# First FFN1 blocks of pair 1 ahead of w1's second half, one transfer for the last weight rows, and LayerNorm of pairs 6 and 7 in the second stage

## The chip, the cores and the metric

The kernel runs on one core of one Trainium2 chip. The metric is device time in microseconds (us) of one execution; the runs of a kernel are given by their median. A profile is one execution recorded by the hardware profiler: its span is the time from the first to the last instruction.

## The reference

Two blocks share one LayerNorm of `A_x` (1 x 2048 x 448, bfloat16) and are added to it; `B_x` is not used.

```python
x  = A_x
xn = layernorm(x)                                   # over 448, eps 1e-5
return x + A(xn, wqkv, w_phi, wo) + B(xn, w1, w2)

# A: linear attention, 16 heads of 28, softmax feature maps
q, k, v = split(xn @ wqkv)
pq, pk  = q @ w_phi, k @ w_phi                      # per head
phi_q   = concat(softmax(pq), softmax(-pq))
phi_k   = concat(softmax(pk), softmax(-pk))
kv, z   = sum_s phi_k v, sum_s phi_k
o       = (phi_q kv) / (phi_q z + 1e-6)
A       = o @ wo
# B: feed-forward, 448 -> 1792 -> 448
B       = silu(xn @ w1) @ w2
```

## The kernel before

The 2048 tokens are cut into 8 **pairs** of 256 tokens. Tokens 2i and 2i+1 of a pair lie in the two tiles t = 0 and 1, on the same partition. Every matmul over the 448 columns contracts seven blocks of 64 rows, and each runs on one half of TensorE's rows: tile 0 on partitions 0 to 63, tile 1 on partitions 64 to 127, both halves at once (`mm_448`, L497). So each weight must be present in both halves. A load (`load_main`, L566) brings rows 0 to 383 as three slots of 128 partitions. `swap` (L575) then copies each half's 64 partitions to the other half, slots 3 to 5, on ScalarE (ACT) or VectorE (DVE). The last 64 rows, 384 to 447, the **tail**, go to slot 6 of both halves by two transfers of 64 rows (`load_tail`, L569).

The work has three stages, which TensorE runs through as one stream:

1. LayerNorm of all pairs (`ln_pair`, L672: bn_stats L621, aggregate L629, ve L635, rstd on POOL L637, normalisation xn L650, then a transpose, for pairs 0 to 3 on TensorE with an eviction by DVE at L668, for pairs 4 to 7 by DMA, L561); the FFN1 blocks of the first pairs (`ffn1_chunk`, L692; 14 blocks of 128 of the 1792 columns, each unit followed by a silu on ACT); and `fold` (L727), which multiplies w_phi into the q and k weights.
2. `k_macro` (L791) for each pair: k matmul, exponentials on ACT, v matmul, v copy (L800), sums Sk and reciprocals Rk on DVE, product phik on POOL (L808); `q_group` (L829), which takes four pairs at a time; and the accumulation of kv (L812). The second group of pairs, 4 to 7, is first read by `q_group` at the fifth pair. At the end, DVE forms KVZ (L854, L855, L862), with a mask of heads.
3. The rest of FFN1, attention output, FFN2 and wo, pair by pair, then the output.

In stage one the first two pairs go as follows. FFN1 blocks 0 to 7 are done for pair 0 alone, since w1 arrives in pieces: w1_0 (columns 0 to 255), w1_0b (256 to 511), w1_1 (512 to 1023), w1_2a (1024 to 1407), w1_2b (1408 to 1791), with tails w1_0t (0 to 511, on ACT's queue) and w1_1t (512 to 1791, on SP's queue behind w1_1). Blocks 8 to 13 are done for pairs 0 and 1 together, and after them blocks 0 to 7 of pair 1. On SP's queue follow x2, x3, w_phi, transposed loads of the q and k weights (wT), x4, x6 and wv.

The order of the instructions on each engine is not written out by hand. A **planner** (`_Prog.schedule`, L218) lists operations with an estimated duration, takes the earliest that can start, and among those within 60 ns the one with the lower priority number and then the earlier place in the program. Loads without a predecessor get a due time from a model of the queues: the end of their bytes at 310 (190 for half transfers) bytes per ns, plus 1700 ns. The resulting order is fixed; on the chip each engine runs its list in order and waits on semaphores. `odeps` are extra order constraints between operations of one engine. Filler matmuls on a tile of zeros (`warm`, L548) have the lowest priority and go where the planner sees nothing else for TensorE.

Of the kernel before, what the change touches and what calls it, by code (L numbers as in the profile page):

```python
# [144 lines left out]
class _Prog:  # L145
# [72 lines left out]
    def schedule(self):  # L218
# [28 lines left out]
        plan = {}  # L247
# [6 lines left out]
        while loads["sp"] or loads["act"]:  # L254
            live = [e for e in ("sp", "act") if loads[e] and loads[e][0][2] <= now]
            nxt = [loads[e][0][2] for e in ("sp", "act") if loads[e] and loads[e][0][2] > now]
            if not live:
                now = min(nxt)
                continue
            cap = [190.0 if ops[loads[e][0][0]].half or ops[loads[e][0][0]].name == "wT_dt" else 310.0 for e in live]  # L260
            rates = [min(c, 310.0 * c / sum(cap)) for c in cap]
            step = min(min(loads[e][0][1] / r for e, r in zip(live, rates)), min(nxt) - now if nxt else 1e18)
            now += step
            if now > 2350.0 and not stalled:
                stalled = True
                now += 900.0
            for e, r in zip(live, rates):
                q = loads[e][0]
                q[1] -= step * r
                if q[1] <= 1.0:  # L270
                    plan[q[0]] = now + 1700.0
                    loads[e].pop(0)

        ndeps = [len(o.deps) + len(o.odeps) for o in ops]
# [90 lines left out]
def bass_parallel_sum__linear_kernel_hedgehog__dense_activation_silu__prompt_kernel(  # L365
# [20 lines left out]
    with es:  # L386
# [141 lines left out]
                                                           base=DH - 1, channel_multiplier=-1),  # L528
             reads=[mtmp[:]], writes=[maskh[:]], name="mask2")
        P.cur_prio = 2  # L530
        for r in range(2):
            P.op("dve", 150, lambda e, r=r: e.tensor_copy(mask2[64 * r:64 * r + 56, :], maskh[0:56, 0:2]),  # L532
                 reads=[maskh[0:56, 0:2]], writes=[mask2[64 * r:64 * r + 56, :]], name="mask3")
        for r in range(2):
            kvz_ones = KVZ[64 * r:64 * r + 56].rearrange("p s g h c -> p (s g) h c")[:, :, :, DH + 1]
            m2 = mask2[64 * r:64 * r + 56]
            P.op("dve", 150, lambda e, k=kvz_ones, m2=m2: e.tensor_copy(k, m2[:, None, :].broadcast_to([56, 8, 2])),  # L537
                 reads=[m2], writes=[kvz_ones], name="kvz1")
        wpad = W_sb[:, :, 0:QW].rearrange("p k (j f) -> p k j f", f=64)[:, :, :, 56:64]
        P.op("pool", d_pool(KB * 64), lambda e: e.memset(wpad, 0.0), writes=[wpad], name="wpad")  # L540

# [3 lines left out]
        zz = sb("zz", [128, 512], BF16)  # L545
        for c0, c1 in ((0, 32), (32, 512)):
            P.op("dve", 450 + (c1 - c0) * 0.3, lambda e, c0=c0, c1=c1: e.memset(zz[:, c0:c1], 0.0), writes=[zz[:, c0:c1]], name="zz")
        for n, rows, cols, dur in ((12, 128, 512, 430.0), (0, 128, 512, 215.0), (14, 128, 256, 109.0)):  # L548
            for i in range(n):
                mm(banks[5][0:rows, 0:cols], zz[:, 0:rows], zz[:, 0:cols], True, True, "warm")  # L550
                P.ops[-1].dur = dur
        P.cur_prio = 0

        def load(dst, src, nbytes, name, eng="sp", keys_r=(), half=False):
            return P.dma(lambda e: e.dma_start(out=dst, in_=src), nbytes, writes=[dst], name=name, eng=eng, keys_r=keys_r, half=half, dur=580.0)
# [10 lines left out]
        def load_main(dst, src, c0, c1, d0, name):  # L566
            load(dst[:, 0:3, d0:d0 + c1 - c0], src[0:384, c0:c1].rearrange("(k p) f -> p k f", p=128), 384 * (c1 - c0) * 2, name)

        def load_tail(dst, src, c0, c1, d0, name, eng="sp"):  # L569
            for h in range(2):  # L570
                o = load(dst[64 * h:64 * h + 64, d0:d0 + c1 - c0], src[384:448, c0:c1], 64 * (c1 - c0) * 2, name, eng, half=True)
                if eng == "act":
                    o.odeps.add(table_op.id)

        def swap(dst, c0, c1, engs):  # L575
            for h in range(2):
                d, q = dst[64 * h:64 * h + 64, 3:6, c0:c1], dst[64 - 64 * h:128 - 64 * h, 0:3, c0:c1]
                if engs[h] == "act":
                    act(d, q, ACTF.Identity, "swap")
                else:  # L580
                    P.op("dve", d_dve(3 * (c1 - c0), 2), lambda e, d=d, q=q: e.tensor_copy(d, q), reads=[q], writes=[d], name="swap")
# [4 lines left out]
        load_x(1, 2)  # L586
        load_main(w1_sb, B_w1, 256, 512, 256, "w1_0b")
        load_main(w1_sb, B_w1, 512, 1024, 512, "w1_1")
        load_tail(w1_sb[:, 6], B_w1, 512, FF, 512, "w1_1t")
        load_main(w1_sb, B_w1, 1024, 1408, 1024, "w1_2a")  # L590
        load_main(w1_sb, B_w1, 1408, FF, 1408, "w1_2b")
        load_x(2, 3)
        load_x(3, 4)
# [51 lines left out]
        def ln_norm(p, t):  # L645
            sl = p % NXN
            dst = xn_sb[:, sl, :].rearrange("p (k t c) -> p k t c", k=KB, t=2)[:, :, t % 2, :]
            for xs, xn in slots(x_sb[:, t, :], dst, t % 2):
                pool = p >= 4 and t % 2
                o = P.op("pool" if pool else "dve", 150 + _cols(xs) * 1.6 if pool else 120 + _cols(xs) * 0.6, lambda e, xn=xn, xs=xs: e.tensor_scalar(  # L650
                    xn, xs, mv[:, t, 0:1], rstd[:, t:t + 1], ALU.subtract, ALU.mult),
                    reads=[xs, mv[:, t, 0:1], rstd[:, t:t + 1]], writes=[xn], name="xn")
                if t < 2:
                    first_xn.append(o)
                    if not pool and t == 0:
                        o.odeps.add(first_ve[1])
# [15 lines left out]
        def ln_pair(p):  # L672
            t0, t1 = 2 * p, 2 * p + 1
            ln_stats(t0)
            if p == 0:
                ln_rstd(t0, t1)
                ln_stats(t1)
                ln_rstd(t1, t1 + 1)
            else:
                ln_stats(t1)  # L680
                ln_rstd(t0, t1 + 1)
            ln_norm(p, t0)
            ln_norm(p, t1)
            ln_tr(p, 6)
# [80 lines left out]
        swap(w1_sb, 768, 1024, ("act", "dve"))  # L765
        ffn1_chunk(0, 1, 4, 8)
        last_mm[-1].odeps |= {q.id for q in second_tr}
        n0 = len(P.ops)
        swap(w1_sb, 1024, 1408, ("act", "dve"))
        second_ev[0].odeps.add(P.ops[-1].id)  # L770
        n0 = len(P.ops)
        swap(w1_sb, 1408, FF, ("act", "dve"))
        P.ops[-1].odeps |= {q.id for q in second_ev}
        ffn1_chunk(0, 2, 8, FT)
        ln_pair(2)
        ffn1_chunk(1, 1, 0, 8)
        ln_pair(3)
        fold()
        ffn1_chunk(2, 1, 0, 8)
        ln_pair(4)  # L780
        ffn1_chunk(2, 2, 8, FT)
        ffn1_chunk(3, 1, 0, 8)
        ln_pair(5)
        ln_pair(6)
        ln_pair(7)

        def k_unit(p, j, b0, name):
            mm_448([banks[b0 + t][:, 0:D] for t in range(2)], lambda h, k: xnT[:, k, p, :],
                   lambda h, k: W_sb[:, k, KO + (j - 1) * D:KO + j * D], True, True, name + "_mm", okeys_w=("late",) if p == NPAIR - 1 and j == 2 else ())

        def k_macro(p):  # L791
            sl = p % NEK
            k_unit(p, 1, 0, "pk")
            kb = psum[:, 0:1024].rearrange("p (t c) -> p t c", t=2)[:, :, 0:D]
            for s in range(2):
                exp_act(Ek[:, sl, :, s, :], kb, 1.0 if s == 0 else -1.0, "exp_k")
            k_unit(p, 2, 2, "v")
            vb = psum[:, 1024:2048].rearrange("p (t c) -> p t c", t=2)[:, :, 0:D].rearrange("p t (h d) -> p t h d", h=H)
            dstv = vaug[:, sl, :, :, 0:DH]
            P.op("dve", d_dve(896), lambda e: e.tensor_copy(dstv, vb), reads=[vb], writes=[dstv], name="v_ev")  # L800
            for ts in ((0, 2),) if p < NPAIR - 1 else ((0, 1), (1, 2)):
                n = ts[1] - ts[0]
                E3 = Ek[:, sl, ts[0]:ts[1], :, :].rearrange("p t s (h f) -> p (t s h) f", f=DH)
                S3, R3 = Sk[:, sl, 32 * ts[0]:32 * ts[1]], Rk[:, sl, 32 * ts[0]:32 * ts[1]]
                P.op("dve", d_dve(896 * n), lambda e, S3=S3, E3=E3: e.tensor_reduce(S3, E3, AXL.X, ALU.add),  # L805
                     reads=[E3], writes=[S3], name="Sk")
                P.op("dve", d_rec(32 * n), lambda e, S3=S3, R3=R3: e.reciprocal(R3, S3), reads=[S3], writes=[R3], name="Rk")  # L807
                P.op("pool", d_pool(896 * n, 1.77), lambda e, E3=E3, R3=R3, n=n: e.tensor_tensor(  # L808
                    E3, E3, R3[:, :, None].broadcast_to([128, 32 * n, DH]), ALU.mult),
                    reads=[E3, R3], writes=[E3], name="phik")  # L810
# [27 lines left out]
                 writes=[vaug[:, sl, :, :, DH]], name="vaug1")  # L838
        for p in range(NPAIR):
            k_macro(p)  # L840
            if 1 <= p <= 5:
                P.keyw["early"] = exps[-1].id
                late_loads(p - 1)
            q_group(p // 4, p % 4)
            if p in (2, 4, 6):
                k_acc(p - 2, p)
# [275 lines left out]
```

## Time and profile before

| | |
|---|---|
| median of 3 runs | 158.16 us (157.37 to 158.72) |
| profiled execution, its own time | 157.24 us |
| its span | 155.5 us |
| TensorE busy | 150.7 us (97%) |
| VectorE busy | 102.6 us (66%) |
| ScalarE busy | 74.2 us (48%) |
| POOL busy | 63.7 us (41%) |
| granted TensorE clock | 1.00 |
| DMA | 12.11 MB, mean 78 GB/s over the span |

"L490" in the profile is the body of `mm_many`, from which nearly all matmuls are issued; "L483" is `mm`, which issues the fillers and the last FFN2 matmuls; "L508" the transposes on TensorE; "L515" every ACT operation; "L581" the swaps on DVE; "L555" every plain load. A busy TensorE is not one at its peak. Idle time of an engine costs only where another engine waits for it.

### The profile page before, as it was taken

The page shows a single profiled execution, that of the slowest core. Times are in us where ns is not written, and L with a number is a line of the kernel's source. Part 1 is how long each engine was busy: PE and PEld are TensorE (multiplying, and loading weights), DVE is VectorE, ACT ScalarE, POOL GpSimd, SP SyncE. Part 2 cuts the span into 40 slices and gives each one's busy share as a digit, 9 for nine tenths or more (in the row PEclk, how much of TensorE's full clock was granted, in tenths as well). Part 3 has the DMA queues.
Part 4 walks back from the last instruction along what each step waited for, and adds up shares of the span by engine and source line. Part 5 has one row for each costly group of instructions (what it writes and reads, how often), then busy time and mean ns, then how long its engine had stood idle before and what let it go on. Part 6 is the DMA issues. An engine that isn't in the chain of part 4 may idle for free.

```text
span 155.5 us, 6049 instructions
## 1 busy us (share of the span) xinstructions
PE 150.7 (97%) x2751; PEld 98.3 (63%) x2751; DVE 102.6 (66%) x198; ACT 74.2 (48%) x82; POOL 63.7 (41%) x73
## 2 busy tenths in 40 slices
PE   6889999999999999999999999999999999999994
PEld 2378899795444546446878898655555555556553
DVE  5897977995978875889098769667985930022042
ACT  3778757878789688785955566800000000000000
POOL 5320306379388775479601453366146060000000
PEclk9999999999999999999999999999999999999999
DMA  5999678303724223300000083300840143041011
GB/s 152 268 277 115 110 180 249 62 17 69 99 53 139 49 93 95 93 0 6 4 4 4 0 63 63 59 4 0 124 118 4 28 115 98 0 118 63 0 59 59
DMA packets 23353, 12.11 MB, mean 78 GB/s; under 512 B 16160, under 2 KB 23200, under 8 KB 23328
## 3 DMA queue, kind: packets, MB, share of 16 engines
q1 hardware_dynamic: 23168, 11.60, 34.9%
q8 instruction: 21, 0.34, 0.9%
q10 hardware_dynamic: 160, 0.13, 0.3%
q14 instruction: 4, 0.03, 0.1%
HBM read 6.22 MB, written 1.84 MB: 52 GB/s over the span
## 4 chain that ended last, share of the span: by engine, by line
PE 89%; DVE 7%; POOL 2%; issue 1%; POOLq 0%
PE psum L490 84%; PE psum L483 4%; PE psum L508 1%; DVE st L621 1%; POOL rstd L637 1%; DVE KVZ L862 1%; DVE kvs L854 1%; DVE kvs L855 1%; DVE mask L532 1%; DVE xn_sb L650 1%; DVE mv L629 0%; DVE xnT L668 0%; DVE ve L635 0%; DVE KVZ L537 0%; POOL ident L519 0%
## 5 line engine op out<-in xcount | busy, mean ns | idle before, releaser
L490 PE MATMUL psum<-xnT,w_sb 64*128 64x256 bf16 (+1 forms) x1008 | 45.6, 246 | 0.5 <-DVE xn_sb L650 0.5
L490 PEld LDWEIGHTS psum<-xnT,w_sb 64*128 64x128 bf16 x1008 | 39.2, 94 | 5.0 <-ACT w_sb L515 0.6
L515 ACT ACTIVATE ar<-psum 128x896 bf16<-128x896 f32 (+2 forms) x38 | 32.0, 880 | 10.9 <-PE psum L490 10.8
L916 POOL TENSOR_TENSOR scr<-scr 128x384 bf16<-128x384 f32 (+3 forms) x32 | 20.1, 660 | 31.8 <-DVE scr L911 26.0
L808 POOL TENSOR_TENSOR ar<-ar,Rk 128x1792 bf16<-128x1792 bf16 (+1 forms) x9 | 25.8, 2877 | 10.1 <-DVE Rk L807 9.1
L960 DVE TENSOR_TENSOR out_sb<-psum,x_sb 128x448 bf16<-128x448 f32 (+2 forms) x17 | 9.5, 593 | 23.6 <-PE psum L490 20.5
L490 PE MATMUL psum<-ar,xnT 64*128 64x448 bf16 x224 | 22.7, 349 | 0.0
L490 PE MATMUL psum<-w_sb,hT_lo 64*128 64x448 bf16 x224 | 22.3, 349 | 0.0
L515 ACT ACTIVATE eq<-psum 128x1024 bf16<-128x1024 f32 x16 | 15.5, 1025 | 6.1 <-PE psum L490 6.0
L805 DVE TENSOR_REDUCE Sk<-ar 128x64 f32<-128x1792 bf16 (+1 forms) x9 | 16.2, 1804 | 2.5 <-ACT ar L515 2.5
L490 PEld LDWEIGHTS psum<-ar,xnT 64*128 64x128 bf16 x224 | 10.7, 94 | 10.4 <-DVE ar L800 0.4
L911 DVE TENSOR_TENSOR scr<-psum,Gq 128x896 f32<-128x896 f32 x16 | 16.9, 1087 | 0.4
L515 ACT ACTIVATE hT_lo<-psum 128x1024 bf16<-128x1024 f32 x14 | 14.3, 1022 | 5.9 <-PE psum L490 5.9
L490 PE MATMUL psum<-w_sb,ar 64*128 64x448 bf16 x168 | 16.6, 349 | 0.0
L490 PEld LDWEIGHTS psum<-w_sb,hT_lo 64*128 64x128 bf16 x224 | 10.5, 94 | 9.4
L637 POOL TENSOR_TENSOR rstd<-ve,neghalf 128x2 f32<-128x2 f32 (+1 forms) x9 | 6.2, 690 | 21.3 <-DVE ve L635 18.9
L490 PE MATMUL psum<-xnT,ar 64*128 64x512 bf16 x112 | 13.4, 376 | 0.0
L490 PEld LDWEIGHTS psum<-w_sb,ar 64*128 64x128 bf16 x168 | 8.4, 94 | 7.4
L490 PE MATMUL psum<-wo_sb,scr 64*128 64x448 bf16 (+2 forms) x119 | 11.9, 338 | 0.0
L800 DVE CAST ar<-psum 128x896 bf16<-128x896 f32 x8 | 8.6, 1069 | 4.0 <-PE psum L490 4.0
L621 DVE BATCH_NORM_STATS2 st<-x_sb 128x6 f32<-128x448 bf16 x16 | 9.7, 613 | 0.5 <-DMA x_sb<-in_A_x_dram 0.4
L650 POOL TENSOR_SCALAR xn_sb<-x_sb,mv,rstd 128x192 bf16<-128x192 bf16 (+1 forms) x8 | 9.5, 1190 | 0.4
(50 smaller groups left out, 119.4 us busy)
## 6 DMA issues: line engine op xcount, KB each, us to landing
out_dram<-out_sb SPq DMA_DIRECT2D x7, 224.0 KB, 2.2
x_sb<-in_A_x_dram SPq DMA_DIRECT2D x4, 224.0 KB, 5.4
x_sb<-in_A_x_dram SPq DMA_DIRECT2D x2, 448.0 KB, 4.8
w_sb<-in_B_w_dram SPq DMA_DIRECT2D x2, 448.0 KB, 3.6
w_sb<-in_B_w_dram SPq DMA_DIRECT2D x2, 336.0 KB, 3.4
w_sb<-in_B_w_dram SPq DMA_DIRECT2D x2, 288.0 KB, 6.6
w_sb<-in_B_w_dram SPq DMA_DIRECT2D x2, 192.0 KB, 3.4
w_sb<-in_B_w_dram SPq DMA_DIRECT2D x1, 384.0 KB, 6.5
```

The source lines that it names most:

```text
L483: lambda e: e.matmul(dst, lhsT, rhs, start=start, stop=stop, skip_group_check=True),
L490: r = e.matmul(dst, lhsT, rhs, start=start, stop=stop, skip_group_check=True)
L515: return P.op("act", d_act(_cols(src)), lambda e: e.activation(dst, src, func, scale=scale), reads=[src], writes=[dst], table=table, name= ...
L621: o = P.op("dve", 630, lambda e: e.bn_stats(st6[:, t, :], x_sb[:, t, :]), reads=[x_sb[:, t, :]], writes=[st6[:, t, :]], name="bnst")
L637: P.op("pool", 580, lambda e: e.tensor_tensor(r2, v2, nh, ALU.pow), reads=[v2, nh], writes=[r2], name="rstd")
L650: o = P.op("pool" if pool else "dve", 150 + _cols(xs) * 1.6 if pool else 120 + _cols(xs) * 0.6, lambda e, xn=xn, xs=xs: e.tensor_scalar(xn ...
L800: P.op("dve", d_dve(896), lambda e: e.tensor_copy(dstv, vb), reads=[vb], writes=[dstv], name="v_ev")
L805: P.op("dve", d_dve(896 * n), lambda e, S3=S3, E3=E3: e.tensor_reduce(S3, E3, AXL.X, ALU.add), reads=[E3], writes=[S3], name="Sk")
L808: P.op("pool", d_pool(896 * n, 1.77), lambda e, E3=E3, R3=R3, n=n: e.tensor_tensor(E3, E3, R3[:, :, None].broadcast_to([128, 32 * n, DH]), ...
L911: P.op("dve", d_dve(896), lambda e, dsto=dsto, Us=Us, Gs=Gs: e.tensor_tensor(dsto, Us, Gs[:, :, :, :, None].broadcast_to([128, 2, 2, 8, DH ...
L916: P.op("pool", d_pool(_cols(a0), 2.26), lambda e, dst=dst, a0=a0, a1=a1: e.tensor_tensor(dst, a0, a1, ALU.add), reads=[a0, a1], writes=[ds ...
L960: P.op("dve", d_dve(c1 - c0), lambda e: e.tensor_tensor(dst, ob, xs, ALU.add), reads=[ob, xs], writes=[dst], name="out_ev")
```

## The change

- The planner's due time of w1_1, w1_1t, w1_2a, w1_2b, w1_2t, x2 and x3 becomes 2600 ns behind the end of their bytes, instead of 1700.
- The four small copies that make the head mask and the ones of KVZ leave the start. They become `late_masks`, placed behind the third pair's `k_macro` and ordered behind the first v copy.
- Of 14 short fillers, 9 stay.
- `load_tail` makes one transfer of 128 partitions whose source is repeated twice, instead of two of 64. All four uses change: w1_0t, the tail of w1's rest, and those of wv and wo. The tail of w1's rest is cut in two: w1_1t (columns 512 to 1023) behind w1_1, and w1_2t (1024 to 1791) behind w1_2a.
- FFN1 blocks 0 to 7 of pair 1 come ahead of blocks 8 to 13 of pairs 0 and 1. The swaps of columns 1024 to 1791 all go to DVE, ordered behind the eviction of pair 1's transpose. LayerNorm of pair 2 comes after block 11, that of pair 3 after blocks 0 to 3 of pair 2.
- LayerNorm of pairs 6 and 7 is placed behind the first and second `k_macro`, and their normalisation is all on DVE; before, the odd tile's was on POOL.

```diff
-                    plan[q[0]] = now + 1700.0
+                    plan[q[0]] = now + (2600.0 if ops[q[0]].name in ("w1_1", "w1_1t", "w1_2a", "w1_2b", "w1_2t", "x2", "x3") else 1700.0)
...
-        for r in range(2):
-            P.op("dve", 150, lambda e, r=r: e.tensor_copy(mask2[64 * r:64 * r + 56, :], maskh[0:56, 0:2]),
-                 reads=[maskh[0:56, 0:2]], writes=[mask2[64 * r:64 * r + 56, :]], name="mask3")
-        for r in range(2):
-            kvz_ones = KVZ[64 * r:64 * r + 56].rearrange("p s g h c -> p (s g) h c")[:, :, :, DH + 1]
...
-        for n, rows, cols, dur in ((12, 128, 512, 430.0), (0, 128, 512, 215.0), (14, 128, 256, 109.0)):
+        for n, rows, cols, dur in ((12, 128, 512, 430.0), (0, 128, 512, 215.0), (9, 128, 256, 109.0)):
...
         def load_tail(dst, src, c0, c1, d0, name, eng="sp"):
-            for h in range(2):
-                o = load(dst[64 * h:64 * h + 64, d0:d0 + c1 - c0], src[384:448, c0:c1], 64 * (c1 - c0) * 2, name, eng, half=True)
-                if eng == "act":
-                    o.odeps.add(table_op.id)
+            o = load(dst[:, d0:d0 + c1 - c0], src[384:448, c0:c1][None].broadcast_to([2, 64, c1 - c0]), 128 * (c1 - c0) * 2, name, eng)
+            if eng == "act":
+                o.odeps.add(table_op.id)
...
         load_main(w1_sb, B_w1, 512, 1024, 512, "w1_1")
-        load_tail(w1_sb[:, 6], B_w1, 512, FF, 512, "w1_1t")
+        load_tail(w1_sb[:, 6], B_w1, 512, 1024, 512, "w1_1t")
         load_main(w1_sb, B_w1, 1024, 1408, 1024, "w1_2a")
+        load_tail(w1_sb[:, 6], B_w1, 1024, FF, 1024, "w1_2t")
         load_main(w1_sb, B_w1, 1408, FF, 1408, "w1_2b")
...
-                pool = p >= 4 and t % 2
+                pool = 4 <= p < 6 and t % 2
...
         last_mm[-1].odeps |= {q.id for q in second_tr}
-        swap(w1_sb, 1024, 1408, ("act", "dve"))
-        second_ev[0].odeps.add(P.ops[-1].id)
-        swap(w1_sb, 1408, FF, ("act", "dve"))
-        P.ops[-1].odeps |= {q.id for q in second_ev}
-        ffn1_chunk(0, 2, 8, FT)
+        silu_1 = silus[-1]
+        ffn1_chunk(1, 1, 0, 8)
+        for c0, c1, after in ((1024, 1408, silu_1), (1408, FF, silus[-2])):
+            swap(w1_sb, c0, c1, ("dve", "dve"))
+            for o in P.ops[-2:]:
+                o.odeps |= {q.id for q in second_ev}
+        ffn1_chunk(0, 2, 8, 12)
         ln_pair(2)
-        ffn1_chunk(1, 1, 0, 8)
+        ffn1_chunk(0, 2, 12, FT)
+        ffn1_chunk(2, 1, 0, 4)
         ln_pair(3)
         fold()
-        ffn1_chunk(2, 1, 0, 8)
+        ffn1_chunk(2, 1, 4, 8)
...
-        ln_pair(6)
-        ln_pair(7)
...
+        def late_masks():
+            for r in range(2):
+                P.op("dve", 150, lambda e, r=r: e.tensor_copy(mask2[64 * r:64 * r + 56, :], maskh[0:56, 0:2]),
+                     reads=[maskh[0:56, 0:2]], writes=[mask2[64 * r:64 * r + 56, :]], name="mask3").odeps.add(v_evs[0])
...
             k_macro(p)
+            if p < 2:
+                ln_pair(6 + p)
+            elif p == 2:
+                late_masks()
```

More of the change, by code (lines that the diff above doesn't have):

```diff
@@ L530, in bass_parallel_sum__linear_kernel_hedgehog__dense_activation_silu__prompt_kernel @@
         P.cur_prio = 2
-        for r in range(2):
-            P.op("dve", 150, lambda e, r=r: e.tensor_copy(mask2[64 * r:64 * r + 56, :], maskh[0:56, 0:2]),
-                 reads=[maskh[0:56, 0:2]], writes=[mask2[64 * r:64 * r + 56, :]], name="mask3")
-        for r in range(2):
-            kvz_ones = KVZ[64 * r:64 * r + 56].rearrange("p s g h c -> p (s g) h c")[:, :, :, DH + 1]
-            m2 = mask2[64 * r:64 * r + 56]
-            P.op("dve", 150, lambda e, k=kvz_ones, m2=m2: e.tensor_copy(k, m2[:, None, :].broadcast_to([56, 8, 2])),
-                 reads=[m2], writes=[kvz_ones], name="kvz1")
         wpad = W_sb[:, :, 0:QW].rearrange("p k (j f) -> p k j f", f=64)[:, :, :, 56:64]
@@ L767, in bass_parallel_sum__linear_kernel_hedgehog__dense_activation_silu__prompt_kernel @@
         last_mm[-1].odeps |= {q.id for q in second_tr}
-        n0 = len(P.ops)
-        swap(w1_sb, 1024, 1408, ("act", "dve"))
-        second_ev[0].odeps.add(P.ops[-1].id)
-        n0 = len(P.ops)
-        swap(w1_sb, 1408, FF, ("act", "dve"))
-        P.ops[-1].odeps |= {q.id for q in second_ev}
-        ffn1_chunk(0, 2, 8, FT)
+        silu_1 = silus[-1]
[5 more added lines that the diff above has]
+        ffn1_chunk(0, 2, 8, 12)
         ln_pair(2)
-        ffn1_chunk(1, 1, 0, 8)
+        ffn1_chunk(0, 2, 12, FT)
+        ffn1_chunk(2, 1, 0, 4)
         ln_pair(3)
         fold()
-        ffn1_chunk(2, 1, 0, 8)
+        ffn1_chunk(2, 1, 4, 8)
         ln_pair(4)
@@ L789, in k_unit @@
                    lambda h, k: W_sb[:, k, KO + (j - 1) * D:KO + j * D], True, True, name + "_mm", okeys_w=("late",) if p == NPAIR - 1 and j == 2 else ())
+        def late_masks():
+            for r in range(2):
+                P.op("dve", 150, lambda e, r=r: e.tensor_copy(mask2[64 * r:64 * r + 56, :], maskh[0:56, 0:2]),
+                     reads=[maskh[0:56, 0:2]], writes=[mask2[64 * r:64 * r + 56, :]], name="mask3").odeps.add(v_evs[0])
+            for r in range(2):
+                kvz_ones = KVZ[64 * r:64 * r + 56].rearrange("p s g h c -> p (s g) h c")[:, :, :, DH + 1]
+                m2 = mask2[64 * r:64 * r + 56]
+                P.op("dve", 150, lambda e, k=kvz_ones, m2=m2: e.tensor_copy(k, m2[:, None, :].broadcast_to([56, 8, 2])),
+                     reads=[m2], writes=[kvz_ones], name="kvz1")
+        v_evs = []
         def k_macro(p):
@@ L800, in k_macro @@
             P.op("dve", d_dve(896), lambda e: e.tensor_copy(dstv, vb), reads=[vb], writes=[dstv], name="v_ev")
+            v_evs.append(P.ops[-1].id)
             for ts in ((0, 2),) if p < NPAIR - 1 else ((0, 1), (1, 2)):
```

## The prediction

> **What bounds the kernel now.** I read the chain that ended last first, by shares and then in order of time.
>
> ```profile
> PE 89%; DVE 7%; POOL 2%; issue 1%; POOLq 0%
> ...
> 10.23 0.39 DVE xn_sb L650
> 10.62 0.12 issue
> 10.74 1.35 PE psum L490 x42
> 12.09 0.43 PE psum L483 x3
> 12.53 0.39 PE psum L508 x7
> 12.92 0.50 PE psum L490 x14
> 13.42 0.32 PE psum L483 x2
> 13.74 4.69 PE psum L490 x84
> ```
>
> Up to 10.7 us the chain runs through the first LayerNorms; from there TensorE (PE) carries it, apart from the 4.0 us of L854, L855 and L862 at 77.6. L483 are fillers on zeros: 0.43 and 0.32 us in which PE had nothing real to do. Next the busy time by stretch (first FFN1 blocks, rest of stage one, stage two, stage three):
>
> ```profile
> 8.55:13.67 5.12, 4.67 (x125) 3.96 (x125) 3.77 (x12) 4.41 (x5) 0.80 (x1) 1.00 1.27 239
> 13.67:35.65 21.98, 21.98 (x551) 19.75 (x552) 19.31 (x53) 15.85 (x21) 9.07 (x10) 1.00 0.63 122
> 35.65:77.60 41.95, 41.88 (x912) 23.34 (x908) 29.74 (x32) 33.68 (x37) 30.37 (x14) 1.00 0.25 61
> ```
>
> Columns: length, then busy PE, weight loads, VectorE (DVE), ScalarE (ACT), POOL, granted clock, DMA share, GB/s. After 13.67 PE is full (21.98 of 21.98, 41.88 of 41.95). So the end moves by what PE gains or loses in starting that stream, plus any new hole in it. The total of real matmuls does not change.
>
> Third, what the stream waits for at the front: the timeline of ACT and the waits of PE's weight loads between 8 and 14 us.
>
> ```profile
> 9.26 1.58 ACT L515 ACTIVATE w_sb<-w_sb 64x768 bf16<-64x768 bf16 x2 [1.12 <-DMA w_sb<-in_B_w_dram]
> ```
> ```profile
> PEld psum L490 <- ACT w_sb L515: 0.6, 1, 0.6
> ```
>
> FFN1 block 4 of pair 0 could not load weights before 10.71, though the ACT copy it needs ended at 10.10 (9.26 + 0.84) and the DVE copy at 9.7. What was still out is the tail of w1 (rows 384 to 447). Adding issue time and time to landing, transfer by transfer: x0 0.79 + 2.4 = 3.2, w1_0b 2.23 + 4.2 = 6.4, w1_1 2.71 + 6.5 = 9.2, second half of w1_1t 4.12 + 6.5 = 10.6, w1_2a 4.74 + 6.5 = 11.2, w1_2b 5.38 + 6.8 = 12.2, x2 5.91 + 6.9 = 12.8, x3 6.44 + 7.0 = 13.4 us. DMA is the resource of the front, and these times are the only slack there is.
>
> **The change part by part.**
>
> *Masks.* Four DVE copies (2.01 to 3.60, 1.13 + 0.43 us) leave the start. x0 is there at 3.2 and the first bn_stats began at 3.63, so pair 0's chain moves up by 0.43 and its first FFN1 from 8.55 to 8.12. The copies come back behind a v copy of stage two, where DVE is busy 29.74 of 41.95 us; their reader (L862, 80.3 us) is 30 us away. Uncovered they would cost 0.75 us at most.
>
> *Fillers.* Nine stand between the transposes of pair 0 and FFN1 (7.47 to 8.62), three and two in the holes above. The last five go. They are a symptom: alone this is worth nothing.
>
> *Planner.* Due times rise by 0.9 us for the late loads. Going through its rule by hand, PE's order stays blocks 0 to 3 of pair 0, blocks 4 to 6, transposes of pair 1, block 7, and then pair 1's eight blocks where pair 0 and 1's blocks 8 to 13 stood.
>
> *w1's second half on DVE.* ACT loses two copies of 1.15 us, DVE gains two of 0.55. All four (2.2 us) now follow pair 1's eviction and lie under pair 1's blocks, 112 matmuls, 3.3 us (18.86 to 22.16 now). Then pair 2's LayerNorm, 3.67 us from first statistics to last xn (14.20 to 17.87 now), must be through before pair 2's blocks: with all data there xn ends at 18.7 and PE asks at about 21.4. Hidden. Without that cover it is 1.1 us.
>
> *LayerNorm of pairs 6 and 7.* POOL gives up four operations (2 x (1.27 + 1.11) us), DVE takes them at 2 x (0.33 + 0.34) = 1.35 us. The planner picks whatever is ready, so they still run around 33 to 40 us, where DVE now loses 1.8 us waiting for a rstd queued behind POOL's xn. Net about 0. Their reader, the first q group over pairs 4 to 7, comes near 57 us. The xnT transfers keep their place on SP's queue, ahead of w2 (44.4 us).
>
> *Sum with the tails spread as the others are.* w1_1t shrinks from 320 to 128 KB and no longer ends last: block 4 starts when the ACT copy is done, 10.2; blocks 4 to 6 end at 11.5; xn of pair 1 is ready at 11.2, its transposes run to 12.05, the eviction (0.62) to 12.75, and the stream starts at 12.83 instead of 13.67: -0.84 us.
>
> *The tail transfer itself.* This decides the case. Each tail becomes one transfer whose source list starts with a dimension of 2 (the copy repeated) and whose destination starts with 128 partitions. Nothing in the trace has this form. The nearest row is the ACT queue's in the first 12 us, which holds only w1_0t as two transfers of 64 rows:
>
> ```profile
> q1 hardware_dynamic: 3269, 2.67, 84.7%
> q10 hardware_dynamic: 160, 0.13, 4.0%
> ```
>
> 160 packets are 128 rows and 32 more, 16 per transfer: each was cut into 16 shares of four rows, one closing packet each. All other first dimensions here are 64, 112 or 128, which 16 divides too. A cut into equal shares along both first dimensions of the new form allows two. The ends: 16 shares, -0.84 us; or two, so that two of the 16 DMA engines carry all tail bytes. The row shows shares that fit the first dimension of both sides, so I take two.
>
> [...]
>
> Cost of two shares. One engine's load in KB, in queue order: x0 14.3, w1_0 12.3, w1_0t 65.5 (now 8.2), x1 14.3, w1_0b 12.3, w1_1 24.6, w1_1t 65.5 (now 20.5), w1_2a 18.4, w1_2t 98.3, w1_2b 18.4, x2 14.3, x3 14.3. Up to x2 that is 358 against 158 now. The rate of an engine: 14.4 KB/us (231 GB/s over 16 at 8 to 9 us), 17 (q10: 131 KB in 4.0% of 16 x 12 us = 7.7 us), 23.9 (382 GB/s over 16 in the best slices of a lone w2 load at 46 us). I take 17 up to 10 us, while all 16 are full, and 22 behind it, nearer the lone row since the others have run dry. With the first byte at 1.8 us and 0.5 us to land: w1_0t 11.7, w1_1t 13.7, w1_2t 19.0, w1_2b 19.8, x2 20.5 us. Then PE: blocks 0 to 3 wait for w1_0t, 11.8 to 13.6; blocks 4 to 7 and transposes to 15.9; pair 1's blocks to 19.2; blocks 8 to 12 to 23.2. DVE: copies of w1_2b 19.8 to 20.9, pair 2's LayerNorm to 24.6. Transposes of pair 2 are queued on PE ahead of block 13, which waits behind them: transposes to 25.3, block 13 to 26.1. Today the same work is done at 22.16: +3.9. Pair 3's xn, 3.3 us behind pair 2's, ends at 27.9 where PE asks at 27.75, and its transposes stand ahead of the fold and the next blocks; with that and the late wT and x4 loads I add 0.6: **+4.5 us**. The whole at 14.4 KB/us gives x2 at 27.2 and +10.3; at 23.9 x2 at 17.3 and +0.9.
>
> 155.5 + 4.5 = 160.0 us of span. This execution took 157.24, so 161.7 on its scale; the median of the runs, 158.16, lies 0.9 above it, so 162.7 us.
>
> **Rivals.**
>
> *The tails spread over 16 engines and the change does what it says* (ends on the other side). For: twice as many partitions in one transfer, and the same number of rows. Against: the packet count above. 157.3 us; should all of the 2.0 us be recovered in which PE has no real matmul between 7.08 and 13.67 (4.55 of 6.59 us are real), 156.2.
>
> *VectorE becomes the bound of stage two, tails harmless.* A pair there costs DVE 1.08 + 2.02 + 0.55 = 3.65 us of PE's 4.16; LayerNorm of two pairs wholly on DVE is 2 x 3.15 = 6.3 us (two statistics at 0.61, two aggregates at 0.18, ve 0.17, four xn 1.39). If it came between the k steps instead of before them, a late v copy would hold the PSUM banks of the next v matmul from a slip of 1.6 us on (copy ends 39.63, next use 41.2). Four pairs have 4 x 0.5 us free; of the 4.3 left, 1.6 is slack: +2.7, less 0.84: 160.0 us. Against: the planner fills earlier gaps, and POOL's relief.
>
> *Two engines, but slow and uncovered:* the +10.3 case, 168.5 us; the upper end of the likeliest.
>
> **How the numbers follow.** About 1%, 1.6 us, is what a measurement of this kernel can tell from no change. Two engines: 0.80, of which 0.74 slower by over 1% and 0.06 within it (the fast end, +0.9). Spread tails: 0.15, of which 0.06 faster and 0.09 within. VectorE: 0.05, 0.04 slower and 0.01 within. Together 0.06 faster, 0.16 the same, 0.78 slower. The likeliest one's own range is 159.0 to 168.5; with the spread case taken in, 157.0 to 167.5.
>
> **What would show it.** Right: times to landing of w1_0t from 3.8 to near 10 us, w1_2t and x2 over 13 us; PE idle or waiting before the first FFN1 block and before block 8; low GB/s with a long DMA tail between 10 and 20 us; stage two as long as now (42 us). The q10 row would hold 128 + 2 packets for one transfer, or 128 + 16 if spread. Wrong: w1_1t landing before 10 us, the stream starting at 12.8, or a stage two longer by over 1 us with DVE named ahead of PE.

## The result and the profile after

The changed kernel took 170.56 us (median of 6 runs, 169.72 to 172.85) against 158.06 us (157.12 to 158.72) before: ratio 1.082, 95% interval 1.077 to 1.087. The forecast was 162.7 us, its range ended at 167.5. The profiled span grew from 155.5 to 168.7 us. "After" is the changed kernel; its lines differ: loads L547, wT L589, bn_stats L613, rstd L629, xn L642, v copy L803, Sk L809, phik L812.

The chain that ended last, by engine (the page of after), then pieces of it in order of time:

```profile
PE 61%; DVE 17%; SPq 16%; DMA 3%; issue 1%; POOL 0%
```
```profile
4.20 2.41 SPq L547
6.65 1.37 SPq L547
8.07 3.46 SPq L547
...
29.26 4.31 DMA ar<-in_A_wqkv_dram
...
49.52 2.74 DVE xn_sb L642 x2
...
54.77 3.37 DVE xn_sb L642 x2
```

Before, TensorE had 89% of the chain. Two strangers stand in it now: SP's issue of loads up to 29 us, and LayerNorm's normalisation xn at 49 to 58 us. The busy time by stretch says how much each is worth (length, then busy PE, weight loads, DVE, ACT, POOL, granted clock, DMA share, GB/s):

```profile
18.55:20.91 2.36, 0.00 (x1) 0.00 (x1) 1.37 (x3) 0.61 (x1) 0.00 (x0) 1.00 1.35 79
...
53.90:59.20 5.30, 0.01 (x4) 0.01 (x2) 5.23 (x6) 2.10 (x3) 3.21 (x1) 0.83 0.00 0
59.20:63.00 3.80, 3.80 (x22) 1.54 (x24) 3.71 (x4) 0.00 (x0) 0.91 (x1) 0.50 0.67 155
63.00:67.00 4.00, 4.00 (x152) 2.17 (x150) 0.87 (x2) 1.73 (x2) 2.30 (x1) 0.85 0.02 4
...
40.90:90.82 49.92, 44.52 (x912) 23.55 (x908) 38.80 (x47) 33.38 (x37) 27.45 (x12) 0.93 0.22 55
```

Stage two, 40.90 to 90.82, is the same 912 matmuls as 35.65 to 77.60 before. So stage one ends 5.25 us later (forecast +4.5), and stage two is 49.92 instead of 41.95 us long: +8.0, where the forecast had none. Of the 8.0, 5.4 are PE idle (49.92 less 44.52; one hole of 5.3) and 2.6 are longer matmuls (44.52 against 41.88): behind the hole the granted clock is 0.50 and comes back to 1.00 only between 63 and 67 us.

**Stage one.** ACT's queue in the first 12 us, which holds w1_0t alone; SP's loads of w1, of before and of after; then PE's timeline in after (start, length, what; in brackets the idle time before the first of a group and what ended it):

```profile
q10 hardware_dynamic: 130, 0.13, 3.1%
```
```profile
2.23 3.63 SPq L555 DMA_DIRECT2D w_sb<-in_B_w_dram  x6
```
```profile
2.23 9.30 SPq L547 DMA_DIRECT2D w_sb<-in_B_w_dram  x6
```
```profile
10.95 1.74 PE L490 MATMUL psum<-xnT,w_sb 64*128 64x128 bf16 x56 [2.47 <-DMA w_sb<-in_B_w_dram]
13.71 1.35 PE L490 MATMUL psum<-xnT,w_sb 64*128 64x128 bf16 x42 [1.02 <-issue]
...
16.36 2.19 PE L490 MATMUL psum<-xnT,w_sb 64*128 64x128 bf16 x72 [0.31 <-DVE xnT L660]
20.91 5.11 PE L490 MATMUL psum<-xnT,w_sb 64*128 64x128 bf16 x110 [2.36 <-issue]
25.95 0.56 PE L508 MATMUL psum<-ident,xn_sb 128*128 128x128 bf16 x7
```

130 packets (160 before) I read as 128 rows and two closing ones: the tail went out in two shares, as forecast. Between 9 and 12 us the DMA share is 0.14, or 2.2 of the 16 engines, at 47 to 48 GB/s; in before the loads moved 293 GB/s then. New against the forecast are two things. SP needs 9.30 us to issue its six loads of w1, before 3.63. The same six loads with tails in 16 shares (kernel 6 below) take 3.91, so it is the two shares that lengthen the issue; by what means is not shown. x2 and x3 were issued from 11.57 on, in before from 5.91, wT from 14.00, in before from 7.44. And PE stops at 18.55 for 2.36 us inside a block, after 72 of 112 matmuls, with no releaser named.

**Stage two.** All engines of after between 48 and 60 us, the rows that matter:

```profile
48.72 3.21 POOL L812 TENSOR_TENSOR ar<-ar,Rk 128x1792 bf16<-128x1792 bf16 x1 [2.37 <-DVE Rk L811]
49.43 2.82 DVE L642 TENSOR_SCALAR xn_sb<-x_sb,mv,rstd 128x384 bf16<-128x384 bf16 x2
...
54.68 3.45 DVE L642 TENSOR_SCALAR xn_sb<-x_sb,mv,rstd 128x192 bf16<-128x192 bf16 x2
54.84 3.21 POOL L812 TENSOR_TENSOR ar<-ar,Rk 128x1792 bf16<-128x1792 bf16 x1 [2.92 <-DVE Rk L811]
58.06 1.08 DVE L803 CAST ar<-psum 128x896 bf16<-128x896 f32 x1
...
59.20 1.30 PE L490 MATMUL psum<-ar,xnT 64*128 64x448 bf16 x6 [5.29 <-DVE ar L803]
```

Pair 7's four xn run between the steps of `k_macro`. A pair of them takes 2.82 and 3.45 us, single ones up to 2.61 and 3.29 us, where the others take 0.25 to 0.4. Each long one lies beside POOL's phik and ends within 0.1 us of it. The second pair stands ahead of the v copy of pair 2 in DVE's list, the copy comes at 58.06, and PE, which needs the PSUM banks that it empties, waits 5.29 us.

### The profile page after: what moved, and what is told of

Same layout as the page of the kernel before. It is cut to its first block, busy times and chain, and to the rows that moved or that the text cites. A ratio compares the mean times of both kernels' runs of the same rounds, so it can differ in the third digit from the quotient of the medians.

```text
span 168.7 us, 6033 instructions
## 1 busy us (share of the span) xinstructions
PE 152.9 (91%) x2746; PEld 98.6 (58%) x2746; DVE 108.9 (65%) x204; ACT 72.2 (43%) x80; POOL 59.0 (35%) x69
## 4 chain that ended last, share of the span: by engine, by line
PE 61%; DVE 17%; SPq 16%; DMA 3%; issue 1%; POOL 0%
PE psum L490 58%; SPq L547 9%; SPq L589 8%; DVE xn_sb L642 5%; PE psum L483 3%; DMA ar<-in_A_wqkv_dram 3%; DVE ar L572 2%; DVE Sk L809 2%; DVE ar L803 2%; DVE st L613 1%; DVE KVZ L870 1%; DVE kvs L862 1%; DVE kvs L863 1%; POOL rstd L629 0%; DVE mv L621 0%
## 5 line engine op out<-in xcount | busy, mean ns | idle before, releaser
L812 POOL TENSOR_TENSOR ar<-ar,Rk 128x1792 bf16<-128x1792 bf16 (+1 forms) x9 | 25.8, 2874 | 17.6 <-DVE Rk L811 16.6
L490 PE MATMUL psum<-ar,xnT 64*128 64x448 bf16 x224 | 25.1, 376 | 5.4 <-DVE ar L803 5.3
L968 DVE TENSOR_TENSOR out_sb<-psum,x_sb 128x448 bf16<-128x448 f32 (+2 forms) x17 | 9.5, 592 | 23.6 <-PE psum L490 20.5
L515 ACT ACTIVATE hT_lo<-psum 128x1024 bf16<-128x1024 f32 x14 | 14.3, 1023 | 11.8 <-PE psum L490 11.8
L809 DVE TENSOR_REDUCE Sk<-ar 128x64 f32<-128x1792 bf16 (+1 forms) x9 | 16.2, 1800 | 3.2 <-ACT ar L515 3.1
L629 POOL TENSOR_TENSOR rstd<-ve,neghalf 128x2 f32<-128x2 f32 (+1 forms) x9 | 6.3, 699 | 32.2 <-DVE ve L627 29.1
L642 DVE TENSOR_SCALAR xn_sb<-x_sb,mv,rstd 128x384 bf16<-128x384 bf16 (+3 forms) x28 | 13.2, 525 | 0.5 <-POOL rstd L629 0.2
L613 DVE BATCH_NORM_STATS2 st<-x_sb 128x6 f32<-128x448 bf16 x16 | 9.8, 612 | 3.4 <-DMA x_sb<-in_A_x_dram 3.4
L803 DVE CAST ar<-psum 128x896 bf16<-128x896 f32 x8 | 8.7, 1082 | 4.0 <-PE psum L490 4.0
```

The lines of the kernel that those rows point to most:

```text
L490: r = e.matmul(dst, lhsT, rhs, start=start, stop=stop, skip_group_check=True)
L515: return P.op("act", d_act(_cols(src)), lambda e: e.activation(dst, src, func, scale=scale), reads=[src], writes=[dst], table=table, name= ...
L613: o = P.op("dve", 630, lambda e: e.bn_stats(st6[:, t, :], x_sb[:, t, :]), reads=[x_sb[:, t, :]], writes=[st6[:, t, :]], name="bnst")
L968: P.op("dve", d_dve(c1 - c0), lambda e: e.tensor_tensor(dst, ob, xs, ALU.add), reads=[ob, xs], writes=[dst], name="out_ev")
```

## The experiments

Kernel 1 is that of experiment 1, and so on. The kernel before took 157.3 to 157.5 us beside them. Theory at the outset: two separate losses, the transfers of the tails in two shares (stage one) and the xn that meet phik (stage two). Rivals: one loss brings about the other; or it is the amount of work on VectorE.

**1. Tails as two transfers, the rest of the change kept.**

```diff
-            o = load(dst[:, d0:d0 + c1 - c0], src[384:448, c0:c1][None].broadcast_to([2, 64, c1 - c0]), ...)
+            def two(e):      # one operation of the planner, two transfers, one semaphore
+                e.dma_start(out=dst[0:64, d0:d0 + c1 - c0], in_=src[384:448, c0:c1]).then_inc(o.dma_sem, 16)
+                return e.dma_start(out=dst[64:128, d0:d0 + c1 - c0], in_=src[384:448, c0:c1])
+            o = P.dma(two, ...)
```

> The changed kernel, every engine's order unchanged, but each tail is again two transfers of 64 rows. Theory (two separate losses: tails on two DMA engines cost stage one 5.3 us; pair 7's xn on VectorE beside POOL's phik costs stage two 8.0 us): the first k matmul comes back from 40.9 to about 35 us, the stage-two loss stays, 164.5 us (162.5 to 165.5). Rival (stage two suffers only because stage one is late): both losses go, 157.3 us. Rival (the tails are not what is late): 170.5 us.

Measured: 164.81 us, ratio 1.047 (1.043 to 1.052). Stage one is cured (first k matmul at 35.67), stage two is as in after. The timeline of this kernel:

```profile
43.76 2.82 DVE L646 TENSOR_SCALAR xn_sb<-x_sb,mv,rstd 128x384 bf16<-128x384 bf16 x2
...
53.52 0.93 PE L490 MATMUL psum<-ar,xnT 64*128 64x448 bf16 x4 [5.22 <-DVE ar L807]
```

The same long xn and the same wait (5.22 against 5.29), without any late load. The second loss doesn't come from the first.

**2. LayerNorm of pairs 6 and 7 back behind pair 5's, odd tile on POOL; tails as in the change.**

```diff
-            if p < 2:
-                ln_pair(6 + p)
-            elif p == 2:
+            if p == 2:
                 late_masks()
...
         ln_pair(5)
+        ln_pair(6)
+        ln_pair(7)
...
-                pool = 4 <= p < 6 and t % 2
+                pool = p >= 4 and t % 2
```

> The changed kernel with LayerNorm of pairs 6 and 7 back behind pair 5 and its odd tiles on POOL; the tails stay one transfer. Theory of two separate losses: stage one as late as in the changed kernel (first k matmul near 40.9 us), stage two near 42 us again, 162.6 us (161.5 to 164). Rival (stage two suffers only because stage one is late): 168 to 171 us.

Measured: 163.36 us, ratio 1.039 (1.036 to 1.042). This is the loss in stage one by itself: stage two takes 41.9 us again. The first k matmul comes at 42.10, later than in after (40.90), because PE ran slower behind its stop. PE's timeline:

```profile
20.45 6.76 PE L490 MATMUL psum<-xnT,w_sb 64*128 64x128 bf16 x110 [2.39 <-issue]
```

The same 110 matmuls took 5.11 us in after. Here the granted clock was 0.67 from 20.45 to 22 and 0.50 to 24 (0.989 on average over the execution), where after kept 1.00 from 20.91 to 40.90.

**3. Both undone (1 and 2 together).**

> Both undone: tails in two transfers, LayerNorm of pairs 6 and 7 back; the rest of the change stays (masks late, FFN1 order, w1's second half on VectorE, nine fillers). Theory: first k matmul at 34.8 us, 157.3 us, 0.8 us faster than before. Rival (the new FFN1 order or the copies on VectorE also cost): over 158.5 us.

Measured: 157.77 us, ratio 1.003 (0.999 to 1.006). So all of the loss lies in these two parts, and they add: 163.36 - 157.77 = 5.6 us for the tails, 164.81 - 157.77 = 7.0 us for LayerNorm's place and engine, together 12.6 of the 12.8 between after and this kernel. How much of the close sum is chance stays open: the profiled stage one of kernel 2 had a slow stretch that after had not, yet its one run at a mean clock of 1.00 took 163.32 us too. What is left of the change gains nothing; the 0.8 us that were expected of it did not come. PE's timeline in this kernel shows why:

```profile
12.52 2.19 PE L490 MATMUL psum<-xnT,w_sb 64*128 64x128 bf16 x72 [0.31 <-DVE xnT L664]
15.57 5.11 PE L490 MATMUL psum<-xnT,w_sb 64*128 64x128 bf16 x110 [0.87 <-issue]
```

The stream starts at 12.52 instead of 13.67, 1.15 us earlier. The stop after 72 matmuls, at the same matmul as in after, takes 0.87 of it; the first k matmul comes at 35.57 against 35.65.

**4. The kernel before with only the tails as one transfer.**

```diff
-            for h in range(2):
-                o = load(dst[64 * h:64 * h + 64, d0:d0 + c1 - c0], src[384:448, c0:c1], 64 * (c1 - c0) * 2, name, eng, half=True)
...
+            o = load(dst[:, d0:d0 + c1 - c0], src[384:448, c0:c1][None].broadcast_to([2, 64, c1 - c0]), 128 * (c1 - c0) * 2, name, eng)
```

> The kernel before with nothing but the tails made one transfer each (w1_1t as one of 320 KB in all). Theory: about 307 KB on each of two DMA engines up to the end of w1_1t, which lands near 18.5 us; FFN1 block 4 of pair 0 starts there instead of 10.7, the full stream near 21.4 instead of 13.7 us, stage two 42 us as before: 165.5 us (163 to 167). Rival (the tail form is harmless alone): 158 us.

Measured: 166.06 us, ratio 1.056 (1.052 to 1.061). PE's timeline:

```profile
10.30 1.74 PE L490 MATMUL psum<-xnT,w_sb 64*128 64x128 bf16 x56 [1.70 <-DMA w_sb<-in_B_w_dram]
17.66 2.42 PE L490 MATMUL psum<-xnT,w_sb 64*128 64x128 bf16 x42 [5.62 <-DMA w_sb<-in_B_w_dram]
```

Here w1_1t is still whole (320 KB), block 4 waits for all of it, 5.62 us: the edit alone costs 8.6 us (166.06 less 157.47). Part of that is the granted clock, 0.50 from 17.66 to 20.00 (0.979 on average over the execution): the 42 matmuls take 2.42 us, in after 1.35. Inside the change the same transfers cost 5.6 us, a third less. Its cut of that tail and its new FFN1 order may be what hides the rest; no run here separates them.

**5 and 6. The first dimension of the source: 4 or 16 instead of 2,** on kernel 2. The last rows then hold other values (32 or 8 rows of w1, wv and wo repeated), the bytes are the same.

```diff
-src[384:448, c0:c1][None].broadcast_to([2, 64, c1 - c0])
+src[416:448, c0:c1][None].broadcast_to([4, 32, c1 - c0])      # 5
+src[440:448, c0:c1][None].broadcast_to([16, 8, c1 - c0])      # 6
```

> The kernel of the run with LayerNorm of pairs 6 and 7 back (163.4 us, tails one transfer each), every order unchanged, with the source of each tail read as four copies of 32 rows (416 to 447) instead of two of 64: same bytes, same destination, first dimension 4. The values in the tails are other ones. Theory (the shares follow the first dimension, four engines): 32.8 KB per engine for w1_0t and w1_1t, block 4 of pair 0 no later than 11 us, stage one late by at most 1 us, 158.3 us (157.3 to 159.5). Rival (a repeated source, or one transfer over 128 partitions, is slow by itself): 163.4 us.

> As the run with first dimension 4, but 16 copies of 8 rows (440 to 447): same bytes, first dimension 16. The values in the tails are other ones. Theory: 16 shares, 16 closing packets for w1_0t (144 packets on its queue), no loss in stage one, 157.7 us. Rival (the repeat itself costs): 163.4 us or more, since each row is read 16 times.

Measured: 160.27 us with 4 (1.017, 1.007 to 1.028; two runs), 158.12 us with 16 (1.003, 0.998 to 1.007). ACT's queue in the first 12 us, with 4 and with 16:

```profile
q10 hardware_dynamic: 132, 0.13, 3.6%
```
```profile
q10 hardware_dynamic: 144, 0.13, 4.5%
```

128 + 2, 128 + 4, 128 + 16 packets, and 163.36, 160.27, 158.12 us: in these three the number of shares is the first dimension, and the repeated source read in 16 shares costs nothing that can be measured. The case of 4 was expected 2 us lower. PE's timeline there shows where they went, at the same matmul again (2.94 us, with 16 shares 0.88):

```profile
18.03 5.11 PE L490 MATMUL psum<-xnT,w_sb 64*128 64x128 bf16 x110 [2.94 <-issue]
```

**7. Kernel 1 with a short phik in pairs 0 and 1** (28 of 1792 columns are multiplied; DVE's list is unchanged).

```diff
+                m = 32 * n if p >= 2 else 1
...
-                    E3, E3, R3[:, :, None].broadcast_to([128, 32 * n, DH]), ALU.mult),
+                    E3[:, 0:m], E3[:, 0:m], R3[:, 0:m, None].broadcast_to([128, m, DH]), ALU.mult),
```

> The kernel of the run with tails in two (164.8 us), every engine's order unchanged; POOL's phik of pairs 0 and 1 works on 28 of 1792 columns only, so most of it is left out for these pairs. Theory (VectorE's xn is shut out while POOL works on phik): the four xn of pair 7 take 0.3 to 0.5 us each instead of up to 3.3, the 5.2 us wait of TensorE for the v copy goes, 157.6 us (156.8 to 158.5). Rival (VectorE simply has too much work in stage two): over 161 us.

Measured: 158.0 us, ratio 1.002 (0.997 to 1.006). All engines around the same xn:

```profile
43.83 0.23 POOL L817 TENSOR_TENSOR ar<-ar,Rk 128x28 bf16<-128x28 bf16 x1 [2.37 <-DVE Rk L815]
44.54 0.57 DVE L646 TENSOR_SCALAR xn_sb<-x_sb,mv,rstd 128x384 bf16<-128x384 bf16 x2
...
47.74 0.49 DVE L646 TENSOR_SCALAR xn_sb<-x_sb,mv,rstd 128x192 bf16<-128x192 bf16 x2
...
49.30 2.82 PE L490 MATMUL psum<-ar,xnT 64*128 64x448 bf16 x28 [0.21 <-DVE ar L807]
```

With the same instructions in the same order on DVE, the xn take 0.57 and 0.49 a pair instead of 2.82 and 3.46, and PE's wait falls from 5.22 to 0.21 us. From the first k matmul to the end this kernel takes 119.95 us, kernel 1 127.33. Meeting phik is the cause; the rival, DVE's amount of work, falls.

**8. Kernel 1 with LayerNorm of pairs 6 and 7 behind pair 5's, but all on DVE; masks still late.**

> The kernel with tails in two and LayerNorm of pairs 6 and 7 back behind pair 5, but their odd tiles on VectorE as in the change. The planner then puts all xn of pair 7 ahead of the first Sk, so ahead of POOL's first phik. Theory (only the meeting with phik costs): 157.8 us (157 to 158.5), xn at 0.3 to 0.6 us each. Rival (1.4 us more work on VectorE costs by itself): 159 to 160 us.

Measured: 160.04 us, ratio 1.015 (1.008 to 1.023). A miss, and not for the rival's reason. The xn took 0.3 to 0.4 each. All engines of this kernel:

```profile
43.61 3.21 POOL L818 TENSOR_TENSOR ar<-ar,Rk 128x1792 bf16<-128x1792 bf16 x1 [3.85 <-DVE Rk L817]
44.39 2.45 DVE L790 COPY mask<-maskh 56x2 f32<-56x2 f32 x1
...
49.49 3.21 POOL L818 TENSOR_TENSOR ar<-ar,Rk 128x1792 bf16<-128x1792 bf16 x1 [2.67 <-DVE Rk L817]
50.33 2.40 DVE L790 COPY mask<-maskh 56x2 f32<-56x2 f32 x1
...
50.35 2.82 PE L490 MATMUL psum<-ar,xnT 64*128 64x448 bf16 x28 [1.48 <-DVE ar L809]
```

Now it is the mask copies that met phik: two columns on 56 partitions, 2.45 and 2.40 us. In kernel 3 they fell ahead of phik and took 0.49 us together.

**9. Kernel 8 with the mask copies at the start again.**

```diff
+        for r in range(2):
+            P.op("dve", 150, lambda e, r=r: e.tensor_copy(mask2[64 * r:64 * r + 56, :], maskh[0:56, 0:2]), ...
...
-            if p == 2:
-                late_masks()
```

> The change with each tail as two transfers of 64 rows, LayerNorm of pairs 6 and 7 behind pair 5's but wholly on VectorE, and the mask copies at the start, as before. Theory (in the kernel with the same LayerNorm and late masks, 160.04 us, the loss was the two mask copies of 2.45 and 2.40 us beside phik): no copy or xn over 1 us between 35 and 60, and the time falls to 158.0 us (157.2 to 158.6). Rival (LayerNorm of two pairs wholly on VectorE is itself too much for it): 159.5 us or more.

Measured: 157.21 us, ratio 1.000 (0.997 to 1.004). LayerNorm of two pairs wholly on DVE costs nothing there. Of the 2.9 us between the profiled spans of kernels 8 and 9, 1.9 lie behind the first k matmul, where the mask copies met phik; the other 1.0 lie ahead of it (36.07 against 35.07), where kernel 8 has the stop in PE (1.37 us) and kernel 9 has none. DVE's timeline:

```profile
35.95 1.09 DVE L654 TENSOR_SCALAR xn_sb<-x_sb,mv,rstd 128x384 bf16<-128x384 bf16 x4
...
38.93 1.08 DVE L654 TENSOR_SCALAR xn_sb<-x_sb,mv,rstd 128x384 bf16<-128x384 bf16 x4
```

**10. A version: the kernel before with late masks, w1's tail cut in w1_1t and w1_2t (two transfers each), nine fillers and the later due times.** FFN1's order, ACT's copies and LayerNorm stay.

> Kernel before with the mask copies behind a v copy of stage two, w1's tail cut as the change cuts it (each tail as two transfers of 64 rows), nine fillers and the later due times; FFN1's order, ACT's share of w1's copies and LayerNorm of pairs 6 and 7 as before. PE's order is before's, so the 256-wide matmuls of blocks 8 to 13 of pairs 0 and 1 follow block 7, and the 128-wide run of pair 1 does not stand there. Theory (the stop of 0.87 us in the middle of pair 1's blocks comes because PE uses up its instructions twice as fast there): the stream starts near 12.5 instead of 13.67, there is no stop in the middle of a block, the first k matmul comes 0.8 to 1.1 us earlier than 35.65, and the time is 156.5 us (156.0 to 157.0), ratio 0.993. Rival (the stop has to do with the number of the matmul in PE's program or with the time, not with how fast they are used up): a stop of about 0.9 us stays and the time is 157.3 or more. A mask copy that falls beside phik would add about 1.5 us to either and would be seen in its row.

Measured: 156.79 us against 157.29, ratio 0.999 (0.996 to 1.001): no difference that can be told, and the expected 0.993 is outside the interval. PE's timeline:

```profile
12.76 4.76 PE L490 MATMUL psum<-xnT,w_sb 64*128 64x256 bf16 x84 [0.41 <-DVE xnT L661]
...
34.74 2.81 PE L490 MATMUL psum<-ar,xnT 64*128 64x448 bf16 x28
...
43.49 2.82 PE L490 MATMUL psum<-ar,xnT 64*128 64x448 bf16 x28 [0.23 <-DVE ar L805]
...
52.49 1.47 PE L490 MATMUL psum<-xnT,ar 64*128 64x512 bf16 x12 [0.53 <-issue]
```

The front did what was expected: start 12.76, no stop in pair 1's blocks, the first k matmul 0.91 us earlier than before. In this execution, at 157.81 us the slowest of the twelve, it was given back in stage two, partly because a v copy stood behind a late xn (37.18 to 37.88, after a rstd queued behind POOL's xn), and 0.53 us in a stop of the kind seen above, at another place.

## Why the prediction was wrong, and where it was right

The time splits in three terms.

- **Tails: right in cause and place, and in size partly by luck.** Forecast, the difference between two shares and spread ones, 162.7 - 157.3 = 5.4 us; measured 5.6 (kernel 2 less kernel 3) and 5.75 (after less kernel 1). w1_2b landed at 19.5 (19.8 forecast) and x2 at 20.0 (20.5), the copies of w1_2b ran 19.48 to 20.62 (19.8 to 20.9), pair 2's last xn ended at 24.32 (24.6). The prediction's choice of two shares, taken from the packet count of the trace before, is borne out: 130, 132 and 144 packets for source first dimensions of 2, 4 and 16. Not foreseen was how the lateness reaches the end: PE's transposes of pair 2 came at 25.95, 1.6 us behind the xn, because of the 2.36 us stop, which no term of the sum held; and SP's issue of w1's loads took 5.7 us longer, which the prediction had only as part of a 0.6 us allowance. One landing doesn't follow from its own lines: in the order listed, w1_0t ends after 92.1 KB, near 7.7 us at 17 KB/us, not at 11.7; the first FFN1 block, which waited for it, began at 10.95.
- **LayerNorm of pairs 6 and 7: the step that failed.** The prediction said "Net about 0"; it was 7.0 us. It assumed that the planner would still run them around 33 to 40 us. The planner put pair 7's xn at 49 to 58 us (in kernel 1, where stage one is in time, at 44 to 52), where phik runs, and the planner's estimate for an xn, 120 ns + 0.6 ns a column, knows nothing of phik. The prediction's own sign of being wrong, a stage two longer by over 1 us with DVE named ahead of PE, is what the profile shows. The durations that the prediction took for DVE (0.33 + 0.34 us) came from rows where POOL wasn't at phik. The rival "VectorE becomes the bound of stage two" named the right place and the right victim, a late v copy holding PSUM banks, but had it from the amount of work, sized it at +2.7 and gave it 0.05. Its argument against, "POOL's relief", was the wrong way round: what POOL does at that time is what stretches the xn, 2.82 us a pair beside the whole phik and 0.57 beside 28 columns of it (kernel 7). It also had no price for a long PE hole: 2.6 of the 8.0 us is the half clock behind it.
- **The rest: -0.84 forecast, +0.3 measured** (kernel 3, 1.003, interval 0.999 to 1.006). The stream did start early (12.52; 12.83 forecast), but a stop in PE took most of it. The masks, "0.75 us at most", are worth nothing where they miss phik, and where they met it, in kernel 8, they took 4.85 us of DVE and cost about 1.9 net. The trace of before held a sign of this: its first mask copy took 0.93 us, to 2.93, which is where a memset on POOL ended (2.16 + 0.77), and the second took 0.16. That w1's copies on DVE lie hidden was right: in kernel 3 no wait of PE names them.

Which of DVE's instructions does phik stretch? Experiment 7 shows that phik's length sets theirs, and the rows show which: the xn (tensor_scalar), up to 3.29 us beside a phik of 3.21, and the copies of the mask, 2.45 us for two columns, both between SBUF tiles. The v copy (from PSUM) and the reduction Sk keep their 1.03 and 2.02 us while phik runs, as in kernel 10:

```profile
42.63 3.21 POOL L814 TENSOR_TENSOR ar<-ar,Rk 128x1792 bf16<-128x1792 bf16 x1 [3.07 <-DVE Rk L813]
43.55 2.02 DVE L811 TENSOR_REDUCE Sk<-ar 128x64 f32<-128x1792 bf16 x1
...
46.08 1.03 DVE L805 CAST ar<-psum 128x896 bf16<-128x896 f32 x1
46.24 3.21 POOL L814 TENSOR_TENSOR ar<-ar,Rk 128x1792 bf16<-128x1792 bf16 x1 [0.40 <-DVE Rk L813]
```

By what means phik stretches them no run shows. And it is not every POOL instruction that does: while POOL's own xn ran in kernel 3 (39.38 to 41.62), a pair of DVE's xn took 0.76 us and the two mask copies 0.49. Why these were not stretched is open.

What else stays open is PE's stop. Summing the counts of PE's timeline, it comes after 219 matmuls in after and in kernels 1, 2, 3, 5, 6, 7 and 8, and after 981 in kernels 5, 6, 9 and 10. 981 - 219 = 762 is six times 127. The queue that the DMA view of after names q8 instruction carries 21 packets, 0.34 MB, and PE has 2746 matmuls and as many weight loads: if all of it were PE's, it would be some 260 instructions a packet, or 130 matmuls, near the 127. That is my estimate from these rows; none of them shows what a packet holds. The starts of these packets, read in narrow windows of the DMA view, can be set beside the stop. In kernels 1, 3, 6, 7 and 8 PE goes on 2.66 to 2.86 us after the start of the last packet ahead of the stop, whether the stop lasted 0.87 or 1.78 us; in kernel 9 that packet starts at 11.64, PE reaches the place 3.3 us later, and there is no stop. With few shares PE goes on later: 4.28 us after the packet's start in after, 5.28 in kernel 2, 6.01 in kernel 5. That PE waits there for a packet is not shown, since no run moved one. The theory of experiment 10, that the narrow matmuls bring about the stop, isn't enough: kernel 9 has the same 72 narrow matmuls there and loses 0.1 us.

## What to carry to other kernels

Before a VectorE operation on SBUF tiles is moved, look at what POOL does at its new place: beside a phik of 3.21 us an xn took up to 3.29 us here and a copy of two columns 2.45, and the price is what stands behind it in VectorE's list (in after, 5.29 us of PE). Look at the first dimension of a transfer: with the same bytes, 2, 4 and 16 gave 163.36, 160.27 and 158.12 us. Count for a transfer that goes out in few shares not only its own landing but the later loads (x2 landed at 20.0 us instead of 12.8) and the issuing queue (9.30 us for six loads instead of 3.63). A gain at the front is one only when it is still there at a fixed point further on, here the first k matmul.

## What the runs showed of the hardware

- A copy of 56 x 2 elements took 2.40 to 2.45 us beside a POOL multiplication, 0.15 to 0.30 without (kernels 3, 7 and 10).
- After a hole of 5.3 us in PE the granted clock was 0.50 from 59.2 to 63.0 and 0.85 on average over the next 4 us. After stops of 2.36 us (after) and 2.94 us (kernel 5) it stayed 1.00, after one of 2.39 us (kernel 2) it fell to 0.50, so in these three the length of the stop alone doesn't tell.
- SP's issuing of six transfers stretched from 3.63 to 9.30 us when the tails went out in two shares (after); the loads moved 44 to 51 GB/s between 9 and 12 us.
- PE stopped with no releaser named after 219 matmuls of its program (0.87 us in kernel 3, 2.36 in after, 2.94 in kernel 5) and after 981 (0.53 in kernel 10, 0.79 in kernel 9, 1.03 in kernel 5).
